# Global products on half the array, logits in another PSUM bank, and a new order in the slots of the expert part

## The chip, the cores and the metric

The kernel runs on one core of a Trainium2 chip. The core has a matrix engine (TensorE, "PE" in the profile, its weight loads "PEld"), VectorE ("DVE"), ScalarE ("ACT"), GpSimd ("POOL") and SyncE ("SP"). Each engine works through its own list of instructions in the order of the program, and semaphores hold an instruction back until another engine's is done. The metric is the device time of one execution in microseconds (us).

## The reference

Two computations stand one behind the other. The first is attention for 8 batches and 8 heads with 512 local tokens, 32 global tokens and a head size of 64. A global token looks at all 544 keys; a local token looks at the 32 global keys and at local keys no more than 32 positions away.

```python
s_g = scale * np.matmul(q_g, k_all.transpose(0, 1, 3, 2))
out_g = np.matmul(sm(s_g), v_all)
...
s_l = np.concatenate([s_lg, s_ll], axis=-1)      # s_ll is masked to |i - j| <= 32
out_l = np.matmul(sm(s_l), np.concatenate([v_g, v_l], axis=2))
return np.concatenate([out_g, out_l], axis=2)
```

The second takes the 4352 result rows x of 512 values, computes logits for 8 experts, balances them with 8 rounds of row and column scaling, and adds up eight two-layer experts with the weights found:

```python
P = np.exp(logits - logits.max())
for _ in range(8):
    P /= P.sum(1, keepdims=True) + 1e-09
    P /= P.sum(0, keepdims=True) + 1e-09
    P *= N / E
for e in range(E):
    out += P[:, e:e + 1] * (np.maximum(x @ w1[e], 0.0) @ w2[e])
```

## The kernel before

The order of the work on every engine is the order of the code: the kernel writes it out by hand. What decides when an instruction starts is its place on its engine and the semaphores of what it reads, and of the tile whose memory it takes over. PSUM pools hand out their two banks in turn: `ps_mm` (tag "mm"), `ps_sc` ("sc"), and in the first part `ps_tr` ("tr"), in the second `ps_z` ("z").

**First part, up to about 335 us.** The loop at L508 runs 34 steps, s = 0 to 33, each for two heads of a batch. A step forms scores (`st_B`, bank "sc"), their softmax on DVE and ACT (L338, L341), transposes (`st_D1`, `st_D2`, `st_A`, banks "tr" and "sc"), and the attention product of an earlier step (`st_E`, L371): 32 matmuls at L384 with 64 columns of weights each, so that two halves of the array are used, and then a reciprocal rr and a product xn on DVE. Between these parts stand pieces of the first two experts, plain two-layer products that keep PE occupied: `f1` issues a piece of the first layer (`p_l1`, L467, bank "mm", called ph; ACT or DVE takes it out as hT) and `f2` a piece of the second (`p_l2`, L481, bank "mm", called py; ACT takes it out as yst). From step 8 on the end of a step is `st_E`, `f2`, then in some steps more, then `f1`, and the next step begins with an `f1`.

Every odd step from 3 on has one global product, `st_G3` (L421), behind that `f2`: five matmuls of 128x260, in a bank "sc", that multiply the transposed softmax of 4 heads (pgs) by the values of these heads at once. Each head needs only its own block of the 4x4 blocks that come out. Then DVE takes a reciprocal rg (L431) and writes two heads of xgn (L438), and ACT writes two (L441). `st_G4` transposes xgn later. In steps 6, 10, 14 and so on, and once behind the loop, `logits` (L450) forms the logits pl of four tiles of tokens in a bank "mm", 16 small matmuls, which DVE copies to lg.

**Second part, from about 363 us.** The other six experts use a scheme that saves products: a layer is cut into four blocks, and seven block products, m1 to m7, are combined with sums. A `Slot` (L872) is a quarter of the first layer for 1024 tokens: its products go into the banks pa ("mm"), pc and pb ("sc"). `m1` writes pa, and ACT copies pa into pc (L907), where `m2` adds to it. `m4` closes pa with a relu on ACT (L915), `m2` closes pc with a relu on ACT (L911), `m3` closes pb with a sum and relu on DVE (`relu_sum`, L899); `m6` and `m7` are copied out of pa by ACT (L920, L929), and `c22` is a further `relu_sum`. A `Unit` (L781) is the second layer for 256 tokens, in a z tile: `sums` and the reads `r1`, `r2`, `r7` are DVE's (L796, L834; in the first expert's stage `r1` and `r2` are ACT's). `run_slot` (L940) puts together one slot: `a` is the new slot, `p` the one before it, whose last products are still due, `x` the unit that was begun one slot earlier and `y` the new one. While there are no units yet (the first slots), `fill` issues the pieces that are left of the first part (py and ph, bank "z"). There are 102 slots. At the end `run_slot(None)` closes the last slot and unit, and `plain` (L860) computes the last units of the last expert without the scheme: four pairs of tiles zp of eight 512-column matmuls, each taken out by DVE and stored.

Of the kernel before, what the change touches and what calls it, by code (L numbers as in the profile page):

```python
# [11 lines left out]
FP32 = mybir.dt.float32  # L12
# [11 lines left out]
def kernel(  # L24
# [13 lines left out]
    nc = tc.nc  # L38
# [89 lines left out]
    with ExitStack() as att:  # L128
# [292 lines left out]
        def st_G3(b, g):  # L421
            pgs = gs.pop((b, g))
            va, vb = vab[b % 2]
            vz = vgz[b % 2]
            po = ps_sc.tile([P, 512], FP32, tag="sc")
            hs = slice(4 * g, 4 * g + 4)
            for t in range(NJ):
                nc.tensor.matmul(po[:, 0 : 4 * VW], pgs[:, t, :], vb[:, t, hs, :], start=(t == 0), stop=False)  # L428
            nc.tensor.matmul(po[:, 0 : 4 * VW], pgs[:, 4, :], vz[:, 3, hs, :], start=False, stop=True)
            rg = att_wk.tile([P, 1], FP32, tag="rg")  # L430
            nc.vector.reciprocal(out=rg, in_=po[:, Dh : Dh + 1])  # L431
            xg = xgn[b // 4]
            o = slice(W * (b % 4), W * (b % 4 + 1))
            for hh in range(4):
                r = slice(W * hh, W * (hh + 1))
                h = 4 * g + hh
                if hh < 2:
                    nc.vector.tensor_scalar(out=xg[o, Dh * h : Dh * (h + 1)], in0=po[r, VW * hh : VW * hh + Dh],  # L438
                                            scalar1=rg[r, 0:1], scalar2=None, op0=ALU.mult)
                else:  # L440
                    nc.scalar.mul(xg[o, Dh * h : Dh * (h + 1)], po[r, VW * hh : VW * hh + Dh], rg[r, 0:1])  # L441

        def st_G4(hf):
            pt = ps_tr.tile([P, HP, P], FP16, tag="tr")
# [2 lines left out]
            t0 = (GT0 + hf) * P  # L447
            nc.scalar.copy(out=xT[:, :, t0 : t0 + P], in_=pt)

        def logits(t0, nt):  # L450
            pl = ps_mm.tile([P, 512], FP32, tag="mm")
            for t in range(nt):
                for dk in range(DP):
                    nc.tensor.matmul(pl[:, E * t : E * (t + 1)], xT[:, dk, P * (t0 + t) : P * (t0 + t + 1)],
                                     wg_sb[:, dk, :], start=(dk == 0), stop=(dk == DP - 1))
            nc.vector.tensor_copy(out=lg[:, t0 : t0 + nt, :], in_=pl[:, 0 : E * nt].rearrange("p (t e) -> p t e", e=E))  # L456
# [51 lines left out]
        for s in range(NU + 2):  # L508
            b, hp = divmod(s, HP)
            if s < NU and b + 1 < B:  # L510
                if hp == 0:
                    queue = load_qk(b + 1, 0, 4, H)
                if hp == 2:
                    *loads, move = load_v(b + 1)
                    queue += loads
                if hp == 3:
                    if s == 3:
                        part = move()
                        for t in qbd:
                            nc.gpsimd.memset(t, 0.0)  # L520
                    else:
                        queue = [move] + queue
                if s == 4:
                    queue += [lambda: wts.__setitem__(1, [load_w1(1)]), lambda: part(nc.gpsimd, True),
                              lambda: part(nc.gpsimd, False), lambda: wts[0].append(load_w2(0))]
                if s == 5:
                    queue += [lambda: load_g(1, "kgs"), lambda: load_g(1, "qgs")]
                if s == 7:
                    queue += [lambda: wts[1].append(load_w2(1))]
                take = 0 if s == 0 else 2 if s >= 8 and hp < 2 else len(queue)  # L530
                if s == 1:
                    queue += [lambda: part(nc.gpsimd, True), lambda: part(nc.gpsimd, False), load_first]
                    take = len(queue)
                for i, f in enumerate(queue[:take]):
                    f()
                if s == 2:
                    clear_z(1, nc.gpsimd)
                    load_vz(1)
                queue = queue[take:]

            if 8 <= s < 8 + 4 * (E - 2):
                sums_load(s - 8)
            if 8 < s <= 8 + 4 * (E - 2):
                sums_form(s - 9)

            l1, l2 = [], []
            if s >= 5:
                pieces = range(4 * (s - 6) + 2, 4 * (s - 6) + 6)
                l1 = [(i // FT % 2, i // FT // 2, i % FT) if i >= 0 else None for i in pieces]
            if s >= 6:  # L550
                k, hf = divmod(s - 6, 2)
                if k >= 1:
                    l2 = [((k - 1) % 2, (k - 1) // 2, 2 * hf + i) for i in range(2)]
            n1 = n2 = 0

            def f1(eng):
                nonlocal n1
                if n1 < len(l1):
                    if l1[n1]:
                        p_l1(*l1[n1], eng)  # L560
                    n1 += 1

            def f2(eng):
                nonlocal n2
                if n2 < len(l2):
                    p_l2(*l2[n2], eng)
                    n2 += 1

            g_odd = s % 2 == 1 and 3 <= s <= NU + 1
            if g_odd:  # L570
                gb, gg = divmod((s - 3) // 2, 2)
            even = s % 2 == 0 and 2 <= s <= NU
            f1("a")
            if s < NU:
                st_B(s, 0)
            if even:
                st_G1(*divmod((s - 2) // 2, 2))
            if 1 <= s <= NU:
                st_D1(s - 1)
            if s == 3:  # L580
                st_E(1)
            if g_odd:
                st_G2(gb, gg)
            f2("a")
            if s < 7:
                st_B(s, 1)
            if 1 <= s < 5:
                keep_busy(3)
            if 1 <= s:
                st_D2(s - 1 if s <= NU else None, s - 2 if s >= 4 else 0 if s == 3 else None)  # L590
            if 7 <= s < NU:
                st_B(s, 1)
            f1("a")
            if s < 7:
                st_A(s + 1)
            if s == 4:
                st_D2(None, 1)
            if s == 1 or s == 2:
                transpose_g(0, *(("qgs",) if s == 1 else ("kgs", Sg)))
            f1("v")  # L600
            if s < NU:
                st_B(s, 2)
            if s == 0:
                cast_g("qgs")
                cast_g("kgs")
            if s + 1 < NU and s >= 7:
                st_A(s + 1)
            if s == 2:
                st_E(0)
            if 3 <= s <= NU:  # L610
                st_E(s - 1)
            f2("a")
            if s >= 6 and (s - 6) % 4 == 0:
                logits(NJ * ((s - 6) // 4), NJ)
            if g_odd:
                st_G3(gb, gg)
            if s == 8:
                transpose_g(1, "kgs")
                transpose_g(1, "qgs")
            if s == 18:  # L620
                st_G4(0)
            f1("v")
            if 1 <= s < 5:
                keep_busy(2)
        logits(NJ * (B - 1), NJ)


        fac = float(E) / float(NTOK)
# [49 lines left out]
        tail_run(2)  # L678
        st_G4(1)
        tail_run(2)  # L680
        logits(GT0, NT - GT0)
        tail_run(1)
        sk_max0()
        tail_run(3)
# [5 lines left out]
    with tc.tile_pool(name="tpool", bufs=2) as tpool, \  # L690
# [166 lines left out]
                if self.e == E - 1:  # L857
                    store(self.m, self.c[0], nc.sync)

        def plain(u, last):  # L860
            order = sorted(range(FT), key=lambda fk: (fk % HF == HF - 1, fk))
            for j in range(2):
                for d0, d1 in ((0, H2), (H2, 3 * P), (3 * P, D)) if last and j else ((0, D),):
                    z = ps_mm.tile([P, D], FP32, tag="mm", name="zq") if d0 else ps_z.tile([P, D], FP32, tag="z", name="zp")
                    for n, fk in enumerate(order):
                        nc.tensor.matmul(z[:, d0:d1], u.a[2 * j + fk // HF][:, fk % HF, :], work["last"][:, fk, d0:d1],  # L866
                                         start=(n == 0), stop=(n == FT - 1), skip_group_check=True)
                    o = u.o(j)[:, d0:d1]
                    nc.vector.scalar_tensor_tensor(out=o, in0=z[:, d0:d1], scalar=u.p[j], in1=o, op0=ALU.mult, op1=ALU.add)
# [70 lines left out]
        def run_slot(a, jobs=()):  # L940
# [14 lines left out]
            if x is None:  # L955
                fill(1)
            if a is not None and p is None:
                fill(some)
            do(x, "m4", "m5", "r2", "r7")
            if x is None:  # L960
                do(p, "m4", "m3")
            do(a, "m2")
            if x is not None:
                do(p, "m4", "m3")
            do(y, "sums", "m1")
            do(a, "m6")
            do(x, "m3", "r1")
# [72 lines left out]
                if q == NQ or f == HF - 1:  # L1040
                    push(k, q)
        final, units = units, []
        run_slot(None)
        for i, u in enumerate(final):
            plain(u, i == len(final) - 1)


# [28 lines left out]
```

## Time and profile before

| what | us |
|---|---|
| median of 3 runs | 1017.83 (1014.74 to 1019.41) |
| the profiled execution | 1014.45 |
| its span, first to last instruction | 1012.7 |
| PE busy | 994.9 (98%) |
| DVE busy | 778.5 (77%) |
| ACT busy | 632.9 (62%) |
| POOL busy | 300.6 (30%) |

A row of the timeline gives the start in us, the duration in us, the engine, the line, the operation, what is written and read by the program's names, the shape and how many such instructions follow each other. A bracket at its end gives the idle time of the engine before it and what ended that; waits under 0.15 us have no bracket. The duration of a matmul includes its way through the array, so matmuls overlap in these rows, and it is the distance between starts that tells how fast PE goes. Rows that merge several instructions span from the start of the first to the end of the last. A row of busy times by stretch gives the stretch, its length, the busy time and count of PE, PEld, DVE, ACT and POOL, then PE's granted clock, the share of the DMA engines and GB/s.

### The profile page before, as it was taken

What the parts mean: (1) busy time and instruction counts of PE and PEld (TensorE: products, weight loads), DVE (VectorE), ACT (ScalarE), POOL (GpSimd) and SP (SyncE); (2) the same over time, 40 slices, a digit from 0 to 9 for tenths busy, and PEclk for the clock granted to TensorE, in tenths of its full rate; (3) what the DMA queues carried; (4) which work ended last, traced back from release to release, by engine and by line L of the source; (5) the groups of instructions that cost most, each with busy time, mean ns of one, the idle gap of its engine ahead of it and who ended that gap; (6) DMA issues with size and microseconds to landing.
All of it is one profiled execution on the core that took longest, in us unless ns stands there. A gap on an engine that the chain in (4) does not pass through costs nothing.

```text
span 1012.7 us, 22301 instructions
## 1 busy us (share of the span) xinstructions
PE 994.9 (98%) x8788; PEld 644.5 (64%) x8788; DVE 778.5 (77%) x1889; ACT 632.9 (62%) x1342; POOL 300.6 (30%) x366
## 2 busy tenths in 40 slices
PE   7899999999999999999999999999999999999997
PEld 4656566656565555666666666676767676766764
DVE  7866666666664664889999888997889999888885
ACT  5877777777774566765555555557765555555551
POOL 9648877887760112111111111111111111100000
PEclk8999999999999999999999999999999999999999
DMA  9999999999852297554443333565664533123043
GB/s 169 180 165 197 226 220 208 203 194 228 208 150 84 90 254 167 156 146 115 115 115 74 73 73 74 126 196 138 161 149 119 115 75 86 47 66 74 1 105 125
DMA packets 135882, 138.42 MB, mean 137 GB/s; under 512 B 54432, under 2 KB 107872, under 8 KB 133728
## 3 DMA queue, kind: packets, MB, share of 16 engines
q0 software_dynamic: 105696, 87.32, 49.1%
q1 hardware_dynamic: 29520, 49.34, 15.0%
q8 instruction: 69, 1.13, 0.5%
q10 hardware_dynamic: 560, 0.33, 0.1%
q14 instruction: 37, 0.30, 0.1%
HBM read 144.20 MB, written 39.58 MB: 181 GB/s over the span
## 4 chain that ended last, share of the span: by engine, by line
PE 94%; DVE 3%; ACT 1%; issue 1%; DMA 0%; ACTq 0%; DVEq 0%
PE z L800 29%; PE pa L895 17%; PE ph L467 12%; PE py L481 11%; PE pb L895 9%; PE pc L895 5%; PE po L384 2%; PE zp L866 1%; PE sc L331 1%; PE ptw L350 1%; PE pk L299 1%; DVE ms L338 1%; PE po L428 1%; DVE Pl L347 1%; PE tgx L360 1%; PE pq L299 1%
## 5 line engine op out<-in xcount | busy, mean ns | idle before, releaser
L800 PEld LDWEIGHTS <-hs 128*128 128x128 f16 x2264 | 220.7, 98 | 92.8 <-issue 1.1
L800 PE MATMUL z<-w2e,hs 128*128 128x256 f16 x1304 | 195.6, 273 | 0.9 <-DVE oy L834 0.9
L800 PE MATMUL z<-v,hs 128*128 128x256 f16 x960 | 144.0, 273 | 0.0
L467 PE MATMUL ph<-xT,w1e 128*128 128x512 f16 (+1 forms) x576 | 129.6, 367 | 2.1 <-DVE lg L456 1.4
L481 PE MATMUL py<-w2e,hT 128*128 128x512 f16 x544 | 128.2, 379 | 0.4 <-DVE hT L472 0.4
L821 ACT COPY z<-z 128x256 f32<-128x256 f32 x98 | 35.0, 357 | 142.0 <-PE z L800 142.0
L895 PEld LDWEIGHTS <-w1e 128*128 128x128 f16 x960 | 86.5, 97 | 57.5 <-issue 1.3
L895 PE MATMUL pa<-t,s 128*128 128x512 f16 x384 | 114.2, 379 | 0.2 <-ACT s L920 0.2
L716 POOL DMA_DIRECT2D w1e<-in_moe_w_dram x24 | 17.4, 732 | 306.2 <-PE pa L895 229.9
L341 ACT ACTIVATE Pu<-ms,mx 128x160 f16<-128x160 f32 x256 | 92.3, 424 | 22.9 <-DVE mx L338 20.2
L834 DVE SCALAR_TENSOR_TENSOR oy<-z,lg,oy 128x512 f32<-128x512 f32 x128 | 95.8, 749 | 7.4 <-ACT oy L839 5.2
L796 DVE TENSOR_TENSOR hs<-hs 128x512 f16<-128x512 f16 x224 | 94.9, 423 | 8.2
L338 DVE CUSTOM_DVE_ANT_0 ms<-sc,mask 128x160 f32<-128x160 f32 x256 | 69.9, 320 | 36.7 <-PE sc L333 34.5
L899 DVE CUSTOM_DVE_ANT_0 hx<-pb,s 128x512 f16<-128x512 f32 x96 | 65.9, 686 | 40.0 <-ACT s L929 31.8
L716 POOL DMA_DIRECT2D w2e<-in_moe_w_dram x24 | 19.8, 830 | 242.7 <-PE z L800 212.4
L911 ACT ACTIVATE hs<-pc 128x512 f16<-128x512 f32 x96 | 57.2, 596 | 52.7 <-PE pc L895 52.6
L467 PEld LDWEIGHTS <-w1e 128*128 128x128 f16 x576 | 53.9, 98 | 52.6 <-issue 2.9
L899 DVE CUSTOM_DVE_ANT_0 hs<-pb,s 128x512 f16<-128x512 f32 x96 | 65.8, 686 | 27.3 <-ACT s L929 26.9
L895 PEld LDWEIGHTS <-s 128*128 128x128 f16 x720 | 65.6, 98 | 29.9 <-issue 1.8
L481 PEld LDWEIGHTS <-hT 128*128 128x128 f16 x544 | 50.0, 98 | 51.8 <-issue 0.5
L472 DVE TENSOR_SCALAR hT<-ph 128x512 f16<-128x512 f32 x58 | 40.1, 692 | 47.7 <-PE ph L467 46.4
L929 ACT COPY s<-pa 128x512 f32<-128x512 f32 x102 | 59.8, 586 | 12.3 <-PE pa L895 1.1
(196 smaller groups left out, 1971.4 us busy)
## 6 DMA issues: line engine op xcount, KB each, us to landing
ys<-yd SPq DMA_DIRECT2D x68, 256.0 KB, 3.4
yd<-yst SPq DMA_DIRECT2D x16, 1024.0 KB, 5.6
pw<-in_moe_w_dram POOLq DMA_DIRECT2D x24, 512.0 KB, 10.3
kept<-psum POOLq DMA_DIRECT2D x24, 512.0 KB, 4.7
s<-kept POOLq DMA_DIRECT2D x12, 768.0 KB, 9.2
v<-kept POOLq DMA_DIRECT2D x12, 768.0 KB, 8.8
w1e<-in_moe_w_dram POOLq DMA_DIRECT2D x12, 512.0 KB, 5.3
w2e<-in_moe_w_dram POOLq DMA_DIRECT2D x12, 512.0 KB, 6.6
```

What stands on the lines that cost most here:

```text
L338: nc.vector.tensor_tensor_reduce(out=ms[:, ii, :], in0=sc[:, SW * ii : SW * (ii + 1)], in1=mask[:, mi, :], scale=-scale, scalar=BIG, op0=A ...
L341: nc.scalar.activation(out=d["Pu"][:, i, :], in_=ms[:, ii, :], func=AF.Exp, scale=-1.0, bias=d["mx"][:, i : i + 1])
L467: nc.tensor.matmul(ph[:, 0:n], wts[e][0][:, dk, P * fm : P * (fm + 1)], xT[:, dk, c0 : c0 + n], start=(dk == 0), stop=(dk == DP - 1))
L472: nc.vector.tensor_scalar(out=hT[:, fm, 0:n], in0=ph[:, 0:n], scalar1=0.0, scalar2=None, op0=ALU.max)
L481: nc.tensor.matmul(py, hT[:, fk, P * c : P * (c + 1)], wts[e][1][:, fk, :], start=(fk == 0), stop=(fk == FT - 1))
L796: nc.vector.tensor_tensor(out=o, in0=x, in1=y, op=op)
L800: nc.tensor.matmul(o, lhs[:, fk, :], rhs[:, fk, :], start=(first and fk == 0), stop=(fk == HF - 1), skip_group_check=True)
L834: nc.vector.scalar_tensor_tensor(out=o, in0=z, scalar=p, in1=o, op0=ALU.mult, op1=ALU.add)
L895: nc.tensor.matmul(o, lhs[:, dk, P * f : P * (f + 1)], rhs[:, dk], start=(first and n == 0 and dk == 0), stop=(dk == HD - 1), skip_group_c ...
L899: nc.vector._custom_dve(TENSOR_ADD_SAT, out=self.to(i, j), in0=self.of(ps), in1=self.of(s), s0=BIG, s1=0.0)
L911: nc.scalar.activation(out=self.to(0, 0), in_=self.of(self.pc), func=AF.Relu)
L929: nc.scalar.copy(out=self.pre3, in_=self.pa)
```

## The change

There are four edits. The global product becomes ten matmuls, five for each half of the array: a half computes two heads from their 64 columns of pgs and their 130 columns of values. It takes a bank of the transposes, and it stands directly behind `st_E`, ahead of the `f2`. The logits of the loop take a bank of the scores. In `run_slot`, `p.m4` goes ahead of `a.m2` where there is a unit, and in the very first slot fewer left pieces are issued ahead of `a.m2`. At the end, `p.m4` and `p.m3` go ahead of `x.r7`, and `x.m3` and `x.r1` go into the first tile of `plain`, behind six of its eight matmuls.

```diff
@@ st_G3
-            po = ps_sc.tile([P, 512], FP32, tag="sc")
-            hs = slice(4 * g, 4 * g + 4)
-            for t in range(NJ):
-                nc.tensor.matmul(po[:, 0 : 4 * VW], pgs[:, t, :], vb[:, t, hs, :], start=(t == 0), stop=False)
-            nc.tensor.matmul(po[:, 0 : 4 * VW], pgs[:, 4, :], vz[:, 3, hs, :], start=False, stop=True)
+            po = ps_tr.tile([P, 512], FP32, tag="tr", name="pog")
+            for t in range(5):
+                for par in range(2):
+                    r, h0 = slice(HB * par, HB * (par + 1)), 4 * g + 2 * par
+                    rhs = vb[:, t, h0 : h0 + 2, :] if t < NJ else vz[:, 3, h0 : h0 + 2, :]
+                    nc.tensor.matmul(po[r, 0 : 2 * VW], pgs[:, t, r], rhs, start=(t == 0), stop=(t == 4))
...
-                    nc.scalar.mul(xg[o, Dh * h : Dh * (h + 1)], po[r, VW * hh : VW * hh + Dh], rg[r, 0:1])
+                    nc.scalar.mul(xg[o, Dh * h : Dh * (h + 1)], po[r, VW * (hh % 2) : VW * (hh % 2) + Dh], rg[r, 0:1])
@@ logits
-        def logits(t0, nt):
-            pl = ps_mm.tile([P, 512], FP32, tag="mm")
+        def logits(t0, nt, pool, tag):
+            pl = pool.tile([P, 512], FP32, tag=tag, name="pl")
@@ the loop over steps
+            if g_odd:
+                st_G3(gb, gg)
             f2("a")
             if s >= 6 and (s - 6) % 4 == 0:
-                logits(NJ * ((s - 6) // 4), NJ)
-            if g_odd:
-                st_G3(gb, gg)
+                logits(NJ * ((s - 6) // 4), NJ, ps_sc, "sc")
...
-        logits(NJ * (B - 1), NJ)
+        logits(NJ * (B - 1), NJ, ps_sc, "sc")
...
-        logits(GT0, NT - GT0)
+        logits(GT0, NT - GT0, ps_mm, "mm")
@@ plain
-        def plain(u, last):
+        def plain(u, last, between=()):
...
                     for n, fk in enumerate(order):
+                        if n == FT - 2 and j == 0:
+                            for f in between:
+                                f()
@@ run_slot
             if a is not None and p is None:
-                fill(some)
+                fill(1)
+                some -= 1
             do(x, "m4", "m5", "r2", "r7")
+            do(p, "m4")
             if x is None:
-                do(p, "m4", "m3")
+                do(p, "m3")
             do(a, "m2")
             if x is not None:
-                do(p, "m4", "m3")
+                do(p, "m3")
@@ the end
-        run_slot(None)
+        p, x = state["slot"], state["unit"]
+        for w in (x.m4, x.m5, x.r2, p.m4, p.m3, x.r7):
+            w()
         for i, u in enumerate(final):
-            plain(u, i == len(final) - 1)
+            plain(u, i == len(final) - 1, (x.m3, x.r1) if i == 0 else ())
```

More of the change, by code (lines that the diff above doesn't have):

```diff
@@ L437, in st_G3 @@
                 if hh < 2:
-                    nc.vector.tensor_scalar(out=xg[o, Dh * h : Dh * (h + 1)], in0=po[r, VW * hh : VW * hh + Dh],
+                    nc.vector.tensor_scalar(out=xg[o, Dh * h : Dh * (h + 1)], in0=po[r, VW * (hh % 2) : VW * (hh % 2) + Dh],
                                             scalar1=rg[r, 0:1], scalar2=None, op0=ALU.mult)
                 else:
-                    nc.scalar.mul(xg[o, Dh * h : Dh * (h + 1)], po[r, VW * hh : VW * hh + Dh], rg[r, 0:1])
+                    nc.scalar.mul(xg[o, Dh * h : Dh * (h + 1)], po[r, VW * (hh % 2) : VW * (hh % 2) + Dh], rg[r, 0:1])
         def st_G4(hf):
```

## The prediction

> **What bounds the kernel now.** I read the page first (busy shares, then the chain that ended last), then the timeline of one slot of the second part, of one odd step of the first part, and of the last 25 us.
>
> ```profile
> span 1012.7 us, 22301 instructions
> PE 994.9 (98%) x8788; PEld 644.5 (64%) x8788; DVE 778.5 (77%) x1889; ACT 632.9 (62%) x1342; POOL 300.6 (30%) x366
> PE 94%; DVE 3%; ACT 1%; issue 1%; DMA 0%; ACTq 0%; DVEq 0%
> ```
>
> PE is the chain: 94% of it, and no DMA. So a change counts by what it takes from PE's stream of instructions, and by waits inside that stream. Most of these are too short for the list of waits and show only as spacing: a 512-column matmul starts 0.2155 us after the one before it, a 256-column one 0.109, and what a gap has above that is a wait.
>
> One slot of the second part:
>
> ```profile
> 603.68 0.59 PE L895 MATMUL pa<-xT,w1e 128*128 128x512 f16 x2
> 603.94 0.59 ACT L929 COPY s<-pa 128x512 f32<-128x512 f32 x1
> 604.11 0.60 PE L800 MATMUL z<-v,hx 128*128 128x256 f16 x4
> 604.42 0.59 ACT L907 COPY pc<-pa 128x512 f32<-128x512 f32 x1
> 604.55 0.60 PE L800 MATMUL z<-w2e,hx 128*128 128x256 f16 x4
> 605.06 0.59 PE L895 MATMUL pc<-xT,w1e 128*128 128x512 f16 x2
> 605.49 0.59 PE L895 MATMUL pa<-t,w1e 128*128 128x512 f16 x2
> 402.09 0.60 PE L800 MATMUL z<-w2e,hx 128*128 128x256 f16 x4
> 402.54 0.59 PE L895 MATMUL pc<-xT,w1e 128*128 128x512 f16 x2
> ```
>
> The four z matmuls from 604.55 are streamed by 604.985; pc (`m2` of the new slot) starts at 605.06, because it accumulates onto what ACT's copy L907 leaves at 605.01. That is a wait of 0.075 in each such slot. In stages of the first expert of a pass it is smaller (402.09 + 0.436 = 402.525 against 402.54, 0.02).
>
> **The change, part by part.**
>
> *Order in the slot.* `p.m4` (two 512-column matmuls, 0.43) moves ahead of `a.m2`. It reads nothing of the copy L907: what it waits for is the previous slot's copy L929, over at 604.53, and its place is now 604.985, so it starts at once with 0.45 to spare. It then covers the copy's end, and `a.m2` starts at 605.42 unhindered. I counted pc's first matmul after z in every slot from 395 to 990: 97 of them, 62 late by 0.075, 5 by 0.06, 27 by 0.02, one by 0.37 (795.57, behind a late ACT), two not at all. 62 x 0.075 + 5 x 0.06 + 27 x 0.02 + 0.37 = **-5.9**. What is late next? ACT runs the two relus in the other order, and pb of `m5` waits for the second: it had 1.2 us or more of slack, and loses about 0.5. The tightest wait after that is `y.m7` on DVE's first sum, which ended at least 0.2 before use, and DVE's chain does not move forward with PE, so 0.13 is left, still more than the 0.05 at which a wait begins to be seen. So all 5.9 should arrive; if that DVE chain caught it halfway, 2.9.
>
> *Filling of the first four slots.* The same 13 pieces are dealt out 4, 3, 3, 3 instead of 8, 2, 2, 1.
>
> ```profile
> 369.46 0.60 PE L467 MATMUL ph<-xT,w1e 128*128 128x256 f16 x4
> 370.31 0.60 PE L467 MATMUL ph<-xT,w1e 128*128 128x256 f16 x4 [0.24 <-ACT yst L484]
> 387.79 0.59 PE L895 MATMUL pb<-xT,w1e 128*128 128x512 f16 x2
> 388.60 0.59 PE L895 MATMUL pa<-t,s 128*128 128x512 f16 x2 [0.22 <-ACT s L920]
> ```
>
> Two short pieces in a row waited for a bank (370.31 - 369.90 = 0.41, and 0.2 at 373); a slot without a piece behind `m5` waited for its copy (388.60 - 388.22 = 0.38). Both go. The fourth slot gets a 0.44 piece instead of a 1.73 one ahead of `p.m4`, and `p.m3` will then wait as it did in the third slot, 0.26. Sum **-0.7** (bounds -1.0 and 0).
>
> *The end.*
>
> ```profile
> 992.41 1.53 DVE L834 SCALAR_TENSOR_TENSOR oy<-z,lg,oy 128x512 f32<-128x512 f32 x2
> 992.55 0.59 PE L895 MATMUL pb<-xT,s 128*128 128x512 f16 x2
> 993.86 0.68 DVE L899 CUSTOM_DVE_ANT_0 hs<-pb,s 128x512 f16<-128x512 f32 x1
> 994.00 0.60 PE L800 MATMUL z<-w2e,hs 128*128 128x256 f16 x4 [0.85 <-DVE oy L834]
> 994.43 13.12 PE L866 MATMUL zp<-w2e,hs 128*128 128x512 f16 x64
> 994.63 0.75 DVE L834 SCALAR_TENSOR_TENSOR oy<-z,lg,oy 128x512 f32<-128x512 f32 x1
> ```
>
> PE stands still from 992.98 to 994.00, since `x.m3` waits for `r7`, over at 993.94. Six zp matmuls (1.29) now go into that hole, but `r7` also moves behind pb's relu_sum: 992.41 + 0.75 for `r2`, then 0.68 from 993.18 (0.2 behind pb's last column), then 0.75 with an overlap of 0.06, so it ends at 994.55 and `x.m3` starts at 994.60. `r1` is over 1.38 after that start (994.63 + 0.75 - 994.00), at 995.98, and the second zp bank is the one that `r1` reads: it starts at 996.03. Before it started at 994.43 + 8 x 0.2155 = 996.15. Of 1.02 us of hole only **-0.1** arrives (bounds 0 and -1.0).
>
> *Logits in a bank of the scores.*
>
> ```profile
> 129.12 1.90 PE L481 MATMUL py<-w2e,hT 128*128 128x512 f16 x8
> 130.86 0.54 PE L454 MATMUL pl<-wg_sb,xT 128*128 128x8 f16 x16
> 131.06 0.59 ACT L484 COPY yst<-py 128x512 f32<-128x512 f32 x1 [0.28 <-PE py L481]
> 131.69 0.38 PE L467 MATMUL ph<-xT,w1e 128*128 128x512 f16 x1 [0.28 <-DVE lg L456]
> 327.29 1.89 PE L481 MATMUL py<-w2e,hT 128*128 128x512 f16 x8 [0.40 <-DVE hT L472]
> ```
>
> The 16 small matmuls take 0.40, so ph could start at 131.26. It starts at 131.69, just after the copy of py is over (131.65): with pl in a "mm" bank, ph takes py's bank. Out of that pool ph gets a bank long free. 0.43 in five steps, 0.2 in step 18 (transposes cover part), 0.55 behind the loop (327.29): **-2.9**. The "sc" bank that pl takes was read by DVE before.
>
> *The global product.* Two halves of the array run beside each other in the rows of the attention product:
>
> ```profile
> 201.10 0.19 PE L384 MATMUL po<-va,pw 128*64 128x65 f16 x1
> 201.57 0.20 PE L384 MATMUL po<-vgz,pg 128*64 128x65 f16 x2
> 201.71 1.90 PE L481 MATMUL py<-w2e,hT 128*128 128x512 f16 x8
> 202.51 0.69 DVE L389 TENSOR_TENSOR xn<-po,rr 128x512 f16<-128x512 f32 x1
> 203.44 0.61 PE L428 MATMUL po<-vb,pgs 128*128 128x260 f16 x4
> 204.00 1.89 PE L467 MATMUL ph<-xT,w1e 128*128 128x512 f16 x8
> 205.06 0.63 ACT L441 ACTIVATE xgn<-po,rg 32x64 f16<-32x64 f32 x2 [0.83 <-PE ph L467]
> ```
>
> From 201.10 to 201.57 thirty of 65 columns start, 0.031 a pair. Ten of 130 in five pairs are then 0.30 (0.27 to 0.56, if nothing overlapped) against 204.00 - 203.44 = 0.56. The change of form behind the 64-column matmuls (0.1, from 201.61 to 201.71) is paid once in either order. By PE alone that is -0.26 a step.
>
> But the reads of the product move with it, ahead of the copy of py on ACT. Step 7 shows that chain without py in it:
>
> ```profile
> 58.42 0.69 DVE L389 TENSOR_TENSOR xn<-po,rr 128x512 f16<-128x512 f32 x1
> 59.03 0.16 DVE L431 RECIPROCAL rg<-po 128x1 f32<-128x1 f32 x1
> 59.22 0.56 DVE L438 TENSOR_SCALAR xgn<-po,rg 32x64 f16<-32x64 f32 x2
> 59.88 0.63 ACT L441 ACTIVATE xgn<-po,rg 32x64 f16<-32x64 f32 x2 [0.60 <-DVE xgn L438]
> 60.53 0.60 ACT L470 ACTIVATE hT<-ph 128x512 f16<-128x512 f32 x1
> ```
>
> xn, rg, two writes of xgn on DVE, then ACT's two (which wait for DVE's last, in every one of the 16), then ACT's next: 1.42 after xn's end. In step 21 xn ends at 203.20, so the copy of py runs from 204.62 to 205.21; before it ran at 203.65. Behind it waits the first ph of the next step, which takes py's bank, two allocations on. By PE's stream that ph is due at 201.71 + 0.30 + 1.73 + 0.86 = 204.60; it will start at 205.25. Before it started at 204.00 + 0.86 = 204.86. So each such step gets **slower by 0.39**, whatever the product costs (up to 0.95). The offset from xn's end is the same in the eleven odd steps 9 to 29; step 31, where xn ends earlier, loses 0.24: 11 x 0.39 + 0.24 = **+4.5**. Steps 3, 5 and 7 have no py and keep up to 0.35 each; PE waits for other engines there soon after, which may swallow it, so I take -0.4 of 0 to -1.0. Step 33 changes by less than 0.1. The queues of SP and POOL keep their order; loads of vb, which wait for the product, may start 1.9 earlier.
>
> The Trainium skill, "TensorEngine Tiling (Array Packing)", section Overview, offers up to 2x for a side of 64 or less; the trace of before agrees for L384, and by that rule alone sixteen products would bring 16 x 0.28, 4.5 less. The same page, section PSUM Bottleneck, says that tiling does not speed the reading of PSUM, which may become the limit; the chain above is that case, and by it the sum is the one below.
>
> **Sum.** -5.9 - 0.7 - 0.1 - 2.9 + 4.5 - 0.4 = -5.5. The profiled execution took 1014.45 (its span and 1.75 around it) and would take 1008.9; the median of the runs is 1017.83, 3.4 above it, and nothing here touches that difference, so the forecast is 1017.83 - 5.5 = **1012.3**.
>
> **Rivals.**
>
> *The half-array product pays in full.* If the copy of py were not held, the +4.5 goes and 12 x 0.26 = 3.1 comes: -13.1, 1004.7. For it: PE is the bound. Against it: the program's order on ACT. The Trainium skill, "TensorE: Matmul & The Clock Gate", section "Architectural detail", calls ScalarE's queue a strict FIFO; no row here shows a later ACT instruction pass an earlier one.
>
> *The slot's gain is caught by DVE.*
>
> ```profile
> 500.00:600.00 100.00, 100.00 (x684) 66.53 (x682) 87.88 (x156) 56.28 (x114) 11.31 (x16) 1.00 0.41 93
> ```
>
> DVE, the third pair here, is busy 87.88 of 100 us, and its sums could become the next wait. Half of 5.9 would be left: -2.6, 1015.2. Against it: at 6.07 a slot DVE would still be idle for 11%.
>
> *Slower: ACT's copy L929 holds `p.m4`.* In the new place `p.m4` and all behind it wait for it. It begins to cost when that copy ends more than 0.45 later than at 604.53, and decides from 0.56 on. Were ACT behind by one copy (0.59), 97 slots would lose 0.14 each, 13.6, and no longer the 5.9: +7.7 instead of -5.9, +8.1 in all, 1025.9. Against it: ACT is the fourth pair, 56.28 busy, and only one slot in 97 (795) shows that copy late.
>
> **How the numbers follow.** About 0.5%, 5.1 us, is what a measurement of this kernel can tell from no change. Forecast 0.66 (its own range 1009 to 1015.5, mostly the spread of the runs shown, 1014.74 to 1019.41), full pay 0.12, caught by DVE 0.15, held by L929 0.07. The forecast lies 0.4 beyond the 5.1, so a little over half of it counts as faster: 0.38 + 0.12 = 0.50; 0.28 + 0.15 = 0.43 the same; 0.07 slower. The range takes in the forecast and the DVE case, most of 0.81: 1007.5 to 1016.5.
>
> **What would show it.** Right: pc starts with no gap behind `p.m4`; slots are 6.07 apart instead of 6.15; in steps 9 to 29 the yst copy follows xgn on ACT and a ph idles about 0.65 behind it; ph follows pl at once; PE idles about 0.3 ahead of the last `x.m3` and 0.55 ahead of the second zp. Wrong: a yst copy ahead of xgn, slots still at 6.15, or gaps ahead of `y.m7`.

## The result and the profile after

The changed kernel takes 1009.29 us in the median (8 runs, 1007.61 to 1011.86), the kernel before 1014.39 beside it (8 runs, 1013.49 to 1019.79). The ratio is 0.9937 with a 95% interval of 0.9914 to 0.996: 5.1 us or 0.5% faster. The forecast was 1012.3, with 5.5 us to gain. The profiled execution of the changed kernel took 1010.12.

The page of the changed kernel (span; busy time, share and count of each engine; the shares of the chain that ended last; one costly group of instructions, with its busy time and mean duration in ns, then the idle time of PE just before them and what ended it):

```profile
span 1008.4 us, 22463 instructions
PE 986.0 (98%) x8868; PEld 640.4 (64%) x8868; DVE 776.8 (77%) x1889; ACT 632.4 (63%) x1342; POOL 300.6 (30%) x366
PE 88%; DVE 5%; POOL 2%; DMA 2%; ACT 2%; issue 1%; SPq 0%; ACTq 0%; POOLq 0%; DVEq 0%
L468 PE MATMUL ph<-xT,w1e 128*128 128x512 f16 (+1 forms) x576 | 131.2, 367 | 6.2 <-ACT yst L485 5.9
```

PE is still the chain, but with 88% of it instead of 94%. The shares of DMA and POOL come from a load that landed late in this execution (told under e7); the page of the second profile of the same kernel has PE 89%, DVE 7%, ACT 3% and neither of the two. The new wait has a name: `ph` for ACT's copy yst, 5.9 us. The list of waits says how often (total, times, longest; of each wait it counts only a part, as the timeline below shows):

```profile
PE ph L468 <- ACT yst L485: 5.9, 12, 0.5
```

Each of these twelve lies at the end of an odd step, from 9 to 31. Step 21 in the timeline of the changed kernel (the rows of the attention product and of other work are left out):

```profile
204.43 0.39 PE L430 MATMUL pog<-vb,pgs 128*64 128x130 f16 x8
204.66 0.22 PE L430 MATMUL pog<-vgz,pgs 128*64 128x130 f16 x2
204.81 1.90 PE L482 MATMUL py<-w2e,hT 128*128 128x512 f16 x8
...
205.33 0.69 DVE L389 TENSOR_TENSOR xn<-po,rr 128x512 f16<-128x512 f32 x1
205.94 0.16 DVE L432 RECIPROCAL rg<-pog 128x1 f32<-128x1 f32 x1
206.13 0.56 DVE L439 TENSOR_SCALAR xgn<-pog,rg 32x64 f16<-32x64 f32 x2
206.55 1.03 PE L468 MATMUL ph<-xT,w1e 128*128 128x512 f16 x4
206.79 0.63 ACT L442 ACTIVATE xgn<-pog,rg 32x64 f16<-32x64 f32 x2 [0.60 <-PE py L482]
207.44 0.58 ACT L485 COPY yst<-py 128x512 f32<-128x512 f32 x1
...
208.07 1.02 PE L468 MATMUL ph<-xT,w1e 128*128 128x512 f16 x4 [0.50 <-ACT yst L485]
```

The first eight half-array matmuls take 0.23 (204.43 to 204.66), the ten so about 0.28: near the low end of the 0.27 to 0.56 of the prediction, which counted with 0.30. But `yst` follows the two ACT writes of xgn, and these follow DVE's. (The bracket at ACT's xgn names py, whose last matmul ends at 206.71, within 0.02 of DVE's second write. In all 16 odd steps ACT's first write starts 0.09 or 0.10 behind DVE's second, and in steps 31 and 33 it does so before py has ended, so DVE is what it waits for.) The second `ph` was due at 206.55 + 4 x 0.2155 = 207.41 and starts at 208.07, after the copy's end at 208.02: a wait of 0.66.

One slot of the second part, the same place as the slot shown of before:

```profile
598.76 0.27 PE L801 MATMUL z<-w2e,hx 128*128 128x256 f16 x1
598.87 0.59 PE L899 MATMUL pa<-t,w1e 128*128 128x512 f16 x2
599.30 0.59 PE L899 MATMUL pc<-xT,w1e 128*128 128x512 f16 x2
599.74 0.59 PE L899 MATMUL pb<-xT,s 128*128 128x512 f16 x2
```

`p.m4` starts 0.11 after the last z matmul, and pc 0.43 after it, with no gap left.

A step with logits, and the end (both timeline, changed kernel):

```profile
133.08 0.54 PE L455 MATMUL pl<-wg_sb,xT 128*128 128x8 f16 x16
133.48 0.81 PE L468 MATMUL ph<-xT,w1e 128*128 128x512 f16 x3
...
989.26 1.46 PE L870 MATMUL zp<-w2e,hs 128*128 128x512 f16 x6
989.46 0.69 DVE L903 CUSTOM_DVE_ANT_0 hs<-pb,s 128x512 f16<-128x512 f32 x1
990.07 0.74 DVE L835 SCALAR_TENSOR_TENSOR oy<-z,lg,oy 128x512 f32<-128x512 f32 x1
990.86 0.60 PE L801 MATMUL z<-w2e,hs 128*128 128x256 f16 x4
991.29 0.59 PE L870 MATMUL zp<-w2e,hs 128*128 128x512 f16 x2
991.50 0.75 DVE L835 SCALAR_TENSOR_TENSOR oy<-z,lg,oy 128x512 f32<-128x512 f32 x1 [0.69 <-PE z L801]
992.30 1.89 PE L870 MATMUL zp<-w2e,hs 128*128 128x512 f16 x8 [0.41 <-DVE oy L835]
```

`ph` follows the 16 logits matmuls after 0.40. At the end PE has six zp matmuls to do while `relu_sum` and `r7` run on DVE, but waits 0.31 ahead of `x.m3` (989.26 + 6 x 0.2155 = 990.55) and 0.58 ahead of the second zp tile (991.29 + 2 x 0.2155 = 991.72).

**Where the time went.** The distance between the starts of the same two instructions, in one profiled execution of each kernel (us; the kernels beside the first two are those of the experiments, and the last column is a sum from the list of waits in the stretch of step 8 to 32):

| kernel | start to xn of step 7 | to xn of step 8 | to xn of step 32 | to the first pc copy | to the sixth | to the last | to the last zq read | waits of tgx for DVE |
|---|---|---|---|---|---|---|---|---|
| before | 58.42 | 8.90 | 248.81 | 48.41 | 31.07 | 589.91 | 22.96 | 0.8 |
| changed | 60.33 | 8.52 | 250.38 | 47.82 | 30.41 | 584.42 | 22.75 | 0.3 |
| e7, changed again | 59.59 | 8.51 | 250.60 | 47.84 | 30.41 | 584.42 | 22.76 | 0.2 |
| e1 | 57.46 | 8.51 | 243.66 | 47.84 | 30.41 | 584.42 | 22.76 | 1.6 |
| e10, e1 again | 58.96 | 8.51 | 244.18 | 47.84 | 30.41 | 584.42 | 22.76 | 1.3 |
| e2 | 57.55 | 8.51 | 249.75 | 47.83 | 30.41 | 589.83 | 22.83 | 0 |
| e3 | 57.66 | 8.90 | 245.26 | 47.88 | 30.41 | 584.42 | 22.76 | 0 |
| e4 | 59.35 | 8.52 | 252.24 | 48.37 | 30.41 | 584.42 | 22.75 | 0 |
| e5 | 60.16 | 8.52 | 243.79 | 47.83 | 30.41 | 584.43 | 21.88 | 1.0 |
| e9, e5 again | 59.63 | 8.51 | 242.10 | 47.83 | 30.41 | 584.42 | 21.88 | 0 |
| e6 | 60.12 | 8.52 | 246.62 | 47.84 | 30.41 | 584.42 | 22.76 | 1.5 |
| e8 | 60.63 | 9.14 | 244.46 | 47.84 | 30.42 | 584.42 | 21.88 | 0 |

Here tgx is the tile of transposes that PE forms from xn and from Pl, a copy of the softmax columns of the global keys. From the fourth stretch on, the distances repeat to 0.1 us in all kernels that have the same code there. The first 60 us do not (57.46 to 60.33 in the kernels above e8, with little or no difference in code). Nor does the stretch of steps 8 to 32: e1, e10, e5 and e9, which have the same code there, take 242.10 to 244.18, and 242.06 to 242.88 when the waits of the last column are taken off. Why is told under e8.

### The profile page after: what moved, and what is told of

Its sections match the earlier page's. It is cut to its first block, busy times and chain, and to the rows that moved or that the text cites. A ratio compares the mean times of both kernels' runs of the same rounds, so it can differ in the third digit from the quotient of the medians.

```text
span 1008.4 us, 22463 instructions
## 1 busy us (share of the span) xinstructions
PE 986.0 (98%) x8868; PEld 640.4 (64%) x8868; DVE 776.8 (77%) x1889; ACT 632.4 (63%) x1342; POOL 300.6 (30%) x366
## 4 chain that ended last, share of the span: by engine, by line
PE 88%; DVE 5%; POOL 2%; DMA 2%; ACT 2%; issue 1%; SPq 0%; ACTq 0%; POOLq 0%; DVEq 0%
PE z L801 30%; PE pa L899 17%; PE ph L468 11%; PE py L482 9%; PE pb L899 9%; PE pc L899 4%; PE ptw L350 1%; PE zp L870 1%; PE sc L331 1%; DVE ms L338 1%; DMA vgz<-vg 1%; DVE xn L389 1%; DMA vg<-in_v_g_dram 1%; PE po L384 1%; ACT yst L485 1%
## 5 line engine op out<-in xcount | busy, mean ns | idle before, releaser
L919 ACT ACTIVATE hs<-pa 128x512 f16<-128x512 f32 x96 | 57.2, 596 | 46.8 <-PE pa L899 46.8
L471 ACT ACTIVATE hT<-ph 128x512 f16<-128x512 f32 (+1 forms) x86 | 48.0, 558 | 37.4 <-PE ph L468 37.0
```

The costliest lines, as they stand in the source:

```text
L471: nc.scalar.activation(out=hT[:, fm, 0:n], in_=ph[:, 0:n], func=AF.Relu)
L919: nc.scalar.activation(out=self.to(1, 0), in_=self.of(self.pa), func=AF.Relu)
```

## The experiments

### e1: the product stays beside the attention product, its reads go behind the copy of py

```diff
@@ st_G3 is cut in two
                     nc.tensor.matmul(po[r, 0 : 2 * VW], pgs[:, t, r], rhs, start=(t == 0), stop=(t == 4))
+            return po
+
+        def st_G3r(b, g, po):
             rg = att_wk.tile([P, 1], FP32, tag="rg")
@@ the loop over steps
             if g_odd:
-                st_G3(gb, gg)
+                pog = st_G3(gb, gg)
             f2("a")
...
                 logits(NJ * ((s - 6) // 4), NJ, ps_sc, "sc")
+            if g_odd:
+                st_G3r(gb, gg, pog)
```

> The changed kernel, except that the reads of the global product (rg, xgn on DVE and ACT) are issued behind the copy of py, where they stood before the change; the ten matmuls stay behind the attention product. Theory (ACT's copy of py waits behind the reads of xgn and holds the first ph of the next step): the twelve waits of about 0.65 us ahead of ph go, and the product's own gain of about 0.27 a step becomes visible: 7.5 to 8 us less than the changed kernel, ratio to before near 0.986, and a ph that follows ph after 0.2155 us. Rival (the product's new bank or form holds ph, whatever the order of its reads): the waits stay, the time is that of the changed kernel within 1 us.

Measured: 1000.66 us in the median (999.83 to 1002.75), ratio to the kernel before 0.9865 (0.9845 to 0.9885). Timeline of e1, the place that answers to step 21 above:

```profile
197.10 0.39 PE L430 MATMUL pog<-vb,pgs 128*64 128x130 f16 x8
197.33 0.22 PE L430 MATMUL pog<-vgz,pgs 128*64 128x130 f16 x2
197.49 1.90 PE L485 MATMUL py<-w2e,hT 128*128 128x512 f16 x8
...
199.22 1.89 PE L471 MATMUL ph<-xT,w1e 128*128 128x512 f16 x8
199.42 0.59 ACT L488 COPY yst<-py 128x512 f32<-128x512 f32 x1 [0.56 <-PE py L485]
200.03 0.63 ACT L445 ACTIVATE xgn<-pog,rg 32x64 f16<-32x64 f32 x2
```

PE's rows are the same up to `ph`, but `yst` starts 0.2 after the last py matmul is streamed (197.49 + 8 x 0.2155 = 199.21), `xgn` follows it, and eight `ph` run without a hole. Only the order of two groups of reads differs from the changed kernel, and steps 8 to 32 fall from 250.4 and 250.6 to 243.7 and 244.2 us. So the price of the early reads is shown, not only argued. e1 beats both kernels.

### e2: `p.m4` behind `a.m2` again

```diff
             do(x, "m4", "m5", "r2", "r7")
-            do(p, "m4")
             if x is None:
-                do(p, "m3")
+                do(p, "m4", "m3")
             do(a, "m2")
             if x is not None:
-                do(p, "m3")
+                do(p, "m4", "m3")
```

> The changed kernel, except that p.m4 stands behind a.m2 again where there is a unit; the filling of the first slots and the end stay as changed. Theory (the copy L907 held a.m2 for 0.075 us in most slots): 5.5 to 5.9 us more than the changed kernel, ratio to before near 1.000, slots of 6.15 us instead of 6.07. Rival (the slots became shorter because of where the banks fall or of the fills): less than 2 us more.

Measured: 1014.1 us, ratio 1.0003 (0.9983 to 1.0022). From the sixth pc copy to the last it takes 589.83 again instead of 584.42, and the wait ahead of pc is back (timeline of e2; 603.21 + 0.436 = 603.65):

```profile
603.08 0.59 ACT L911 COPY pc<-pa 128x512 f32<-128x512 f32 x1
603.21 0.60 PE L801 MATMUL z<-w2e,hx 128*128 128x256 f16 x4
603.72 0.59 PE L899 MATMUL pc<-xT,w1e 128*128 128x512 f16 x2
```

Without this one edit the other three together bring nothing that can be measured, since what the logits, the filling and the end gain is lost at the global product (the terms are below). The slot order carries the result.

### e3: the old global product, 128x260 in a bank of the scores behind `f2`

```diff
-            po = ps_tr.tile([P, 512], FP32, tag="tr", name="pog")
...
+            po = ps_sc.tile([P, 512], FP32, tag="sc")
+            hs = slice(4 * g, 4 * g + 4)
+            for t in range(NJ):
+                nc.tensor.matmul(po[:, 0 : 4 * VW], pgs[:, t, :], vb[:, t, hs, :], start=(t == 0), stop=False)
+            nc.tensor.matmul(po[:, 0 : 4 * VW], pgs[:, 4, :], vz[:, 3, hs, :], start=False, stop=True)
...
-            if g_odd:
-                st_G3(gb, gg)
             f2("a")
...
+            if g_odd:
+                st_G3(gb, gg)
```

> The changed kernel with the old global product: five matmuls of 128x260 in a bank of the scores, behind the f2 piece, read behind the copy of py. Theory (the moved product loses 0.39 us a step): 4 to 5 us less than the changed kernel, ratio to before near 0.989. Rival (the half-array product pays in full): 3 us more than the changed kernel. It also shows whether the first 60 us, which came out 2 us longer in the changed kernel's profile, are long because of the product.

Measured: 1006.06 us (1003.23 to 1012.68), ratio 0.9929 (0.9902 to 0.9955). In the median that is 2.5 and 3.2 less than in the two sets of runs of the changed kernel, and the intervals of the ratios overlap, so the medians alone do not decide it. The trace does: steps 8 to 32 take 245.26, 5.1 and 5.3 less than in the two profiles of the changed kernel, and no `ph` waits for `yst`. The product as it was moved costs more than the product before. The first 60 us take 57.66 here, but 57.46 and 57.55 in e1 and e2 with the half array, so it is not the product that made them long in the changed kernel's profile.

### e4: the logits of the loop in a bank "mm" again

```diff
-                logits(NJ * ((s - 6) // 4), NJ, ps_sc, "sc")
+                logits(NJ * ((s - 6) // 4), NJ, ps_mm, "mm")
...
-        logits(NJ * (B - 1), NJ, ps_sc, "sc")
+        logits(NJ * (B - 1), NJ, ps_mm, "mm")
```

> The changed kernel with the logits of the loop in a bank mm again. Theory (ph behind pl takes py's bank and waits for its copy): 2.5 to 3 us more than the changed kernel, ratio to before near 0.9965, with waits of 0.43 us between pl and ph. Rival (the wait behind pl was covered by other work of the step): no difference, within 1 us.

Measured: 1011.24 us, ratio 0.9966 (0.9955 to 0.9977). By the ratios that is 2.9 us more than the changed kernel, where 2.5 to 3 was expected (the interval of its first runs overlaps this one, that of e7 does not). The trace shows the wait: `ph` waits again behind the logits (timeline of e4; 132.21 + 0.40 = 132.61):

```profile
132.21 0.55 PE L455 MATMUL pl<-wg_sb,xT 128*128 128x8 f16 x16
133.03 1.89 PE L468 MATMUL ph<-xT,w1e 128*128 128x512 f16 x8 [0.28 <-DVE lg L457]
```

0.42 of wait, where the changed kernel has none; behind the loop 48.37 against 47.82.

### e5: e1 with the end mended

```diff
@@ plain
-                    z = ps_mm.tile([P, D], FP32, tag="mm", name="zq") if d0 else ps_z.tile([P, D], FP32, tag="z", name="zp")
+                    z = ps_mm.tile([P, D], FP32, tag="mm", name="zq") if d0 or (j and between) else ps_z.tile([P, D], FP32, tag="z", name="zp")
...
-                        if n == FT - 2 and j == 0:
+                        if n == FT - 3 and j == 0:
@@ the end
-        for w in (x.m4, x.m5, x.r2, p.m4, p.m3, x.r7):
+        for w in (x.m4, x.m5, x.r2, x.r7, p.m4, p.m3):
```

> The kernel of e1_reads_behind_py, with the end rearranged: r7 is issued ahead of p.m4 and p.m3 again, x.m3 and x.r1 go behind five zp matmuls instead of six, and the second zp tile takes an mm bank instead of the z bank that r1 reads. Theory of the prediction (the changed kernel's end gives its hole back as two waits, about 0.3 us ahead of the last x.m3 and 0.55 us ahead of the second zp): both waits go, the end is about 0.9 us shorter than in e1_reads_behind_py, and the ratio to the kernel before is about 0.9855. Rival (the end is set by the last DVE sums and stores, not by PE): the waits go, but the distance from the second zp to the end of the span grows by as much, ratio 0.9865 as in e1_reads_behind_py.

Measured: 1002.07 us, ratio 0.9874 (0.986 to 0.9887), which does not tell the two theories apart. The trace does (timeline of e5):

```profile
982.52 1.24 PE L875 MATMUL zp<-w2e,hs 128*128 128x512 f16 x5
983.59 0.60 PE L806 MATMUL z<-w2e,hs 128*128 128x256 f16 x4
984.03 0.81 PE L875 MATMUL zp<-w2e,hs 128*128 128x512 f16 x3
984.68 1.89 PE L875 MATMUL zq<-w2e,hs 128*128 128x512 f16 x8
```

Five matmuls, `x.m3`, three, and the second tile follow each other without a hole, and from the last slot to the last zq read it takes 21.88 instead of 22.76: 0.88 less, all of it kept.

### e6: e1 with the half-array product behind `py`

```diff
-            if g_odd:
-                pog = st_G3(gb, gg)
             f2("a")
...
             if g_odd:
-                st_G3r(gb, gg, pog)
+                st_G3r(gb, gg, st_G3(gb, gg))
```

> The kernel of e1_reads_behind_py, but the ten half-array matmuls of the global product stand behind f2 and the logits, where the wide product stood, in the transposes' bank; the reads follow them at once. The order of the reads on DVE and ACT is that of e1_reads_behind_py. Theory (each change between 64-column and 128-column weights costs PE about 0.1 us, and this place adds two such changes a step, while the place beside the attention product adds none): 12 steps x 0.2 = 2.4 us more than e1_reads_behind_py, ratio to the kernel before about 0.989. Rival (changes of form cost nothing, the half array saves the same at any place): the same as e1_reads_behind_py, ratio 0.9865.

Measured: 1005.54 us (1002.0 to 1009.22), ratio 0.9907 (0.9888 to 0.9926). Timeline of e6, the same step:

```profile
201.67 1.90 PE L485 MATMUL py<-w2e,hT 128*128 128x512 f16 x8
203.50 0.42 PE L430 MATMUL pog<-vb,pgs 128*64 128x130 f16 x8
203.75 0.22 PE L430 MATMUL pog<-vgz,pgs 128*64 128x130 f16 x2
203.91 1.90 PE L471 MATMUL ph<-xT,w1e 128*128 128x512 f16 x8
```

py is streamed by 201.67 + 8 x 0.2155 = 203.39, the product starts 0.11 later and `ph` 0.41 after that. From the first matmul of the attention product to the first `ph` it is 203.91 - 201.06 = 2.85 here, 199.22 - 196.59 = 2.63 in e1, and 204.00 - 201.10 = 2.90 in the kernel before. So at the old place the half array is worth 0.05 a step, and the place beside other 64-column work is worth 0.22. Steps 8 to 32, less the waits of the last column, take 245.12, where e1, e10, e5 and e9 take 242.06, 242.88, 242.79 and 242.10: 2.7 more than their mean of 242.46, and 2.4 was expected. The theory holds.

### e7, e9, e10: the changed kernel, e5 and e1 again

> The changed kernel itself, beside the other two on one chip, so that the cost of the early reads is measured against the same runs. Theory (reads of the product ahead of the copy of py cost 11 x 0.66 us of waits ahead of ph): about 6.7 us more than e1_reads_behind_py would be, ratio to the kernel before about 0.993, and in the first 60 us no load of vg that lands late. Rival (the late load of vg in its first profile belongs to the change): po waits for vgz again for about 1 us in step 5.

> The kernel of e5_end_mended again, beside e10_reads_behind_py_again on one chip. Theory (the mended end is worth the 0.9 us that its trace shows between the last slots and the end of the span): median 0.9 us below e10's, if the scatter of the first part allows that to be seen. Rival (nothing): the same median.

> The kernel of e1_reads_behind_py again: median about 0.986 to 0.987 of the kernel before, and 0.9 us above e9_end_mended_again by the theory there, the same by its rival.

The changed kernel took 1008.55 us here (ratio 0.9938, 0.9926 to 0.995), 6.5 above e5 beside it; less e5's 0.88 for the end, the early reads cost 5.6 there, and 7.1 to 7.9 against e10's and e1's medians on two other chips, around the 6.7 expected. In its first profile one load had landed late, and the list of waits showed it:

```profile
PE po L384 <- DMA vgz<-vg: 1.1, 1, 1.1
```

This wait is in no other list but e9's, with 0.8. e7 has the same code and is without it, so it is not the change's. e9 took 1000.42 (ratio 0.9853, 0.983 to 0.9877) and e10 1001.47 (0.9874, 0.9845 to 0.9902): 1.05 less, the expected sign and size, but less than the two intervals can tell apart. For the 0.88 the trace remains the evidence.

### e8: the copy of Pl on ACT instead of DVE

What differs between executions of one kernel in steps 8 to 32? In e6 one step lost 1.5 us in one place. The copy of Pl on DVE in e6 and what GpSimd did meanwhile, and the same copy in e1:

```profile
269.50 2.55 DVE L347 COPY Pl<-Pu 128x256 f16<-128x256 f16 x1
269.62 2.33 POOL L120 TENSOR_TENSOR psum<-pw 128x512 f16<-128x512 f16 x2
272.10 0.29 PE L364 MATMUL tgx<-identity,Pl 128*128 128x128 f16 x2 [1.45 <-DVE Pl L347]
```

```profile
264.45 0.22 DVE L347 COPY Pl<-Pu 128x256 f16<-128x256 f16 x1
```

```diff
-            nc.vector.tensor_copy(out=d["Pl"], in_=d["Pu"][:, :, KW:SW])
+            nc.scalar.copy(out=d["Pl"], in_=d["Pu"][:, :, KW:SW])
```

> The kernel of e5_end_mended, but the copy Pl<-Pu of st_D1 (32 of them in the first part) is ACT's instead of DVE's. In the traces so far this copy takes 0.22 us on DVE where GpSimd is idle and up to 2.55 us where a GpSimd instruction overlaps it, and PE then waits for Pl by 1.0 to 1.5 us at L364, in other steps in each execution. Theory (that collision makes much of the 1 to 3 us by which executions of one kernel differ in the first part): no wait for Pl is left, none of the 32 copies is longer than 0.45 us, and the median is 1 to 2 us below e5_end_mended's on the same chip, with a smaller scatter. Rival (ACT has no room for 32 copies of 0.37 us, 11.8 us in all, ahead of its copies of py and of pgs): new waits for ACT of 0.2 us or more a step, the same median or up to 5 us above.

Measured (on top of e5): 1004.95 us (1004.27 to 1007.23), ratio 0.9902 (0.9881 to 0.9923), 4.5 above e9 on the same chip. The group of these copies on the page's list and the list of waits of e8:

```profile
L347 ACT COPY Pl<-Pu 128x256 f16<-128x256 f16 x32 | 12.6, 393 | 0.0
```

```profile
PE tgx L364 <- ACT Pl L347: 4.6, 5, 1.7
```

All 32 copies now take 0.39 or 0.40, 18 of them beside a TENSOR_TENSOR of GpSimd: the collision with GpSimd is real and is gone. But the time is worse, and the scatter is no smaller (a range of 3.0 us, 3.2 in e9). The list puts 4.4 of its 4.6 us into the first 60 us. e9, however, has 3.0 us of waits ahead of tgx for DVE there, and from the start to xn of step 7 e8 is only 1.0 longer. Step 8 takes 0.63 more, and the largest part, 2.36, lies in steps 8 to 32 (244.46 against 242.10), where the list shows one wait of 0.2. The rows there tell more (timeline of e8):

```profile
188.22 0.72 ACT L408 ACTIVATE Pg<-sg,m 128x544 f16<-128x544 f32 x1 [0.43 <-DVE m L406]
188.69 0.39 PE L360 MATMUL tgx<-identity,xn 128*128 128x128 f16 x4
188.83 0.39 ACT L347 COPY Pl<-Pu 128x256 f16<-128x256 f16 x1
189.28 0.28 PE L364 MATMUL tgx<-identity,Pl 128*128 128x128 f16 x2 [0.21 <-ACT Pl L347]
```

In every second step the copy stands on ACT behind the exponential of the global scores (L408). In eleven of these between steps 8 and 32 the tgx that reads it starts 0.05 or 0.06 after its end, 0.14 to 0.37 later behind the tgx before it than in e9: 2.6 us in all, most of it in waits too short for the list. The theory of the collision holds, the hope for the median falls, and what was measured is the rival's price: ACT has no room for the copy.

## Why the prediction was right

*Order in the slot, -5.9.* -5.5 from the sixth pc copy to the last (584.42 for 589.91), of which e2 gives back 5.41. The mechanism is as told; the size was a little high, since most slots became 0.072 shorter where 0.075 was counted, and 0.017 where 0.02 was. DVE did not catch the gain, nor did `p.m4` wait for L929: from 400 to 985 us no matmul of the changed kernel starts more than 0.04 late behind a 512- or 256-column one.

*Filling, -0.7.* -0.66 (30.41 for 31.07), in every profile; no run takes this edit alone.

*The end, -0.1.* -0.21, of which the slot order gives 0.08 (e2, with the old order, has 22.83) and the end itself 0.13. Both waits are where they were placed, 0.31 and 0.58 for 0.3 and 0.55. e5, which loses both and 0.88 us with them, shows that they were the whole reason.

*Logits, -2.9.* Behind the loop -0.53 (e4's 48.37 to 47.84). In steps 8 to 32, e4 without them takes 252.24; the three profiles with them, less their waits for DVE, 250.08, 250.4 and 249.75, a mean of 2.2 less. Together -2.7.

*The global product, +4.5.* In e4 the product is the only edit in steps 8 to 32: 252.24 against 248.81 - 0.8 = 248.01, +4.2. The two halves of this term stand apart in the other runs: e3, with the old product, takes 245.26; with the new one and late reads it is 242.46 (the mean under e6), so the product by itself brings 2.8 (3.1 was worked out). The changed kernel lies 7.6 above that mean (250.08), and its twelve waits, by the distance between the starts of two ph, are 7.9 together (0.66 or 0.67 in eleven steps, 0.52 in step 31). The chain on ACT is as told, too: 1.42 lies between xn's end and the copy of py, from 206.02 to 207.44. The prediction weighed a rule of the Trainium skill here ("TensorEngine Tiling (Array Packing)", section PSUM Bottleneck): the reading of PSUM is not sped up by tiling and may become the limit. The trace agrees that the reads became no faster: the two on DVE take 0.56 and the two on ACT 0.63 in both kernels, while the matmuls fell from 0.56 to 0.28. But the length of the reads was not the limit, although the prediction took its chain for that case: e1 has the same reads behind the copy of py, and no ph waits. Their place on ACT decided.

*Steps 3, 5 and 7, -0.4.* -0.38 at step 7 (8.51 for 8.90), in all kernels with the half array except e8, and 0 in e3. What steps 3 and 5 brought is lost in the scatter of the first 60 us.

*The sum and its base.* The terms were to sum up to -5.5. As measured they give -5.2, and the medians differ by 5.1. That the sum is closer than its terms is in part luck: the slots brought 0.4 less than forecast, and the product cost 0.3 less. The forecast lay 3.0 above the result all the same, and the step that failed is the last one: 3.4 us were added because the median of the runs shown was 1017.83, with the words that nothing here touches that difference. It was scatter: beside the changed kernel the kernel before had a median of 1014.39 in eight runs, those three among them, near the 1014.45 of the profiled execution. The sum against the profiled execution, 1008.9, lay 0.4 from the measured median.

*The rivals.* That the half array pays in full needed the reads behind the copy of py: it is what e1 is, 1000.66. The two others did not occur.

## What to carry to other kernels

When a product is moved to an earlier place, its readers need not move with it: issue them where their engine would otherwise idle, and behind whatever frees the next bank. A cheaper form of a product is worth most beside work of the same form: here 0.22 of the 0.27 us came from the place. Where single executions differ by as much as the change brings, compare distances between the same instructions stage by stage, and give the base of a forecast its own doubt: here the median of three runs was 3.4 us too high, and the profiled execution was near the later median.

## What the runs showed of the hardware

A DVE copy of 128x256 f16 from SBUF to SBUF took 0.22 us alone and up to 2.55 us beside GpSimd's work (269.50 above). The row shows more than one collision: the copy outlasted two GpSimd instructions in a row, which end at 271.95. In steps 8 to 32 of the eleven profiles with this copy on DVE, it is the only DVE instruction that ever took more than 0.25 us above its usual time, each time beside a GpSimd instruction, and every wait of tgx for DVE there stands behind such a copy. As these meet at other steps in each execution, PE waited between 0 and 1.6 us for DVE ahead of tgx. In e1, e10, e5 and e9 this accounts for most of what made profiles of the same code differ there: 2.1 us between them, 0.8 without these waits. In the changed kernel, e7 and e2, where the waits are 0.3 at most, it is 0.85 and 0.65, so part of the scatter stays open.

The Trainium skill, "SBUF — State Buffer", section "Who interferes with whom", says that DVE and GpSimd, but not ACT, share a pair of ports as an exclusive lock, that a DVE copy can need it, and that the one that comes second blocks fully. The trace agrees that the copy stood still (2.55 for 0.22), and e8 agrees that ACT is not held (0.39 or 0.40 in all 32 copies). Which of the two came first the rows do not show: the record of the long copy starts at 269.50, ahead of GpSimd's at 269.62.
